# The last product of a transformer block, done as two column halves in two PSUM banks

## The chip, the cores and the metric

One core of a Trainium2 chip. The time is device microseconds of one execution, the median of several; in a trace the span from the first to the last instruction is some 2 us shorter. Engines: PE (TensorE) multiplies matrices, DVE (VectorE), ACT (ScalarE) and POOL (GpSimd) work elementwise, SP issues the transfers. PE writes into PSUM, which the kernel declares as 8 banks of 512 float columns. In the views L790 is line 790 of the kernel that ran, and a bracket says how long the engine had been idle before and what ended that.

## The reference, cut to what matters

```python
x = x + ga * _A_ref(h, A_wqkv, A_w_phi, A_wo)      # linear attention
h = _layernorm(x, axis=-1) * (1 + cb) + sb
x = x + gb * _B_ref(h, B_w1, B_w2)                 # relu(h @ w1) @ w2
```

x is 2048 x 576, the hidden layer 4608 wide. The change concerns only the last line: the second layer's product, the gate `gb`, and the residual addition.

## The kernel before: the parts that matter

The 2048 rows are 16 tiles of 128, worked in 8 passes of two. A pass forms its second-layer products in a scheme with partial products, which are summed in PSUM or through scratch copies (`SS`); the columns are in two parts of `HD = 288`. `fin` adds a saved partial sum, multiplies by the gate and adds the residual. Its scratch `yt` has one row of 288 floats for each column part:

```python
def fin(t, k, bank, s):
    c = slice(k * HD, (k + 1) * HD)
    y = yt[:, k, :]
    if s is None:
        dve.tensor_tensor(out=y, in0=PS[:, bank, 0:HD], in1=gb_row[:, c], op=ALU.mult)
    else:
        dve.tensor_tensor(out=y, in0=PS[:, bank, 0:HD], in1=SS[:, s, :], op=ALU.add)
        pool.tensor_tensor(out=y, in0=y, in1=gb_row[:, c], op=ALU.mult)
    pool.tensor_tensor(out=x_sb[:, t, c], in0=y, in1=x_sb[:, t, c], op=ALU.add)
```

The end of the last pass; t and t + 1 are its tiles:

```python
    fin(t + 1, 1, Z, 2)
    prod(X, A22, T4, al)
    fin(t + 1, 0, X, None)            # multiplies into yt[:, 0], POOL adds from there
    sp.dma_start(outf[(t + 1) * P:(t + 2) * P, :], x_sb[:, t + 1, :])
    ...                               # (passes before the last return here)
    rows, z = slice(t * P, (t + 1) * P), yt[:, 1, :]
    sp.dma_start(outf[rows, 0:HD], x_sb[:, t, 0:HD])
    pool.tensor_tensor(out=z, in0=SS[:, 1, :], in1=gb_row[:, HD:D], op=ALU.mult)
    pool.tensor_tensor(out=z, in0=z, in1=x_sb[:, t, HD:D], op=ALU.add)
    prod(Z, A12, B22, al)             # the last product: 18 matmuls of 288 columns
    dve.tensor_tensor(out=yt[:, 0, :], in0=PS[:, Z, 0:HD], in1=gb_row[:, HD:D], op=ALU.mult)
    dve.tensor_tensor(out=x_sb[:, t, HD:D], in0=yt[:, 0, :], in1=z, op=ALU.add)
    sp.dma_start(outf[rows, HD:D], x_sb[:, t, HD:D])
```

The softmax here doesn't subtract the row's maximum and nothing guards it: scores larger than these inputs give would overflow.

## Time and profile before

| | kernel before |
|---|---|
| time, first three runs | 392.11 us (391.75 to 392.55) |
| span of the profiled run | 390.7 us |
| PE busy | 98% |
| start of the last product | 384.42 us |
| end of the last product | 2.37 us after its start |
| last store issued | 3.56 us after its start |
| last instruction | 6.28 us after its start |

PE is full up to the end of the last product, so only the stretch behind it can be shortened by this change.

### The profile page before, as it was taken

The numbers are of one execution on the slowest core, as the hardware profiler recorded it, in microseconds if no ns is written. First come the engines' busy times: TensorE is split into PE (matmuls) and PEld (weight loads), VectorE is DVE, ScalarE is ACT, GpSimd is POOL, SyncE is SP. The second block draws the span as 40 slices with busy tenths as digits, with TensorE's granted clock in tenths as the row PEclk, the third lists the DMA queues.
The fourth block names the chain that finished last, engine by engine and source line by source line (L and its number), as shares of the span: only waits on it lengthen the run. The fifth ranks groups of instructions, "written<-read, shape, count | busy, mean of one in ns | idle before, by whom it ended". The sixth has DMA issues, their size and how long they took to land.

```text
span 390.7 us, 8908 instructions
## 1 busy us (share of the span) xinstructions
PE 383.8 (98%) x3693; PEld 311.7 (80%) x3693; DVE 244.3 (63%) x452; ACT 157.9 (40%) x360; POOL 142.3 (36%) x199
## 2 busy tenths in 40 slices
PE   8999999999999999999999999999999999999995
PEld 4778888878887888788888878887888788878874
DVE  0889998854879746573755567458555664653221
ACT  1798779699531233124213510531143123312510
POOL 2155858741101510740164045306510641072045
PEclk9999999999999999999999999999999999999999
DMA  7999739795732151125313311450143124010001
GB/s 291 418 420 403 274 133 354 178 306 161 189 65 35 47 121 20 35 61 109 35 27 83 80 35 32 107 65 19 47 93 35 24 69 51 18 34 33 3 0 32
DMA packets 49515, 44.36 MB, mean 114 GB/s; under 512 B 39361, under 2 KB 42050, under 8 KB 48706
## 3 DMA queue, kind: packets, MB, share of 16 engines
q1 hardware_dynamic: 49186, 43.59, 39.6%
q8 instruction: 29, 0.48, 0.5%
q10 hardware_dynamic: 288, 0.19, 0.2%
q14 instruction: 12, 0.10, 0.1%
HBM read 27.97 MB, written 6.49 MB: 88 GB/s over the span
## 4 chain that ended last, share of the span: by engine, by line
PE 86%; POOL 6%; ACT 2%; DVE 2%; DMA 2%; issue 1%; SPq 0%; POOLq 0%; DVEq 0%; ACTq 0%
PE PS L683 33%; PE PS L742 29%; PE PS L274 9%; PE PS L410 5%; PE PS L690 5%; POOL wo_sb L637 2%; PE PS L235 2%; PE PS L391 1%; ACT RT L279 1%; POOL RH L754 1%; DMA gatd<-gt 1%; PE PS L324 1%; POOL RT L291 1%; DMA ga_row<-gatd 1%; DVE st L240 1%
## 5 line engine op out<-in xcount | busy, mean ns | idle before, releaser
L683 PE MATMUL PS<-h,R 128*128 128x256 bf16 x1152 | 133.5, 273 | 0.0
L683 PEld LDWEIGHTS <-R 128*128 128x128 bf16 x1152 | 109.8, 98 | 17.5 <-issue 5.1
L742 PEld LDWEIGHTS <-RH 128*128 128x128 f16 x864 | 84.5, 98 | 21.8
L728 POOL TENSOR_TENSOR yt<-yt,gb_row 128x288 f32<-128x288 f32 x23 | 16.8, 731 | 167.0 <-DVE yt L727 167.0
L742 PE MATMUL PS<-R,RH 128*128 128x288 bf16 (+1 forms) x576 | 75.6, 286 | 0.0
L697 ACT ACTIVATE RH<-PS 128x256 f16<-128x256 f32 x72 | 27.7, 384 | 114.0 <-PE PS L690 107.4
L699 DVE SCALAR_TENSOR_TENSOR RH<-PS,RH 128x256 f16<-128x256 f32 x72 | 30.1, 419 | 68.2 <-ACT RH L697 68.2
L279 ACT ACTIVATE RT<-PS,rs 128x576 bf16<-128x576 f32 x64 | 43.0, 750 | 7.5 <-PE PS L274 7.1
L698 ACT ACTIVATE RH<-PS 128x512 f16<-128x512 f32 x72 | 42.9, 595 | 7.8 <-PE PS L683 6.5
L746 ACT ACTIVATE RS<-PS 128x288 f32<-128x288 f32 x24 | 9.9, 411 | 75.9 <-PE PS L742 75.9
L742 PE MATMUL PS<-RT,RH 128*128 128x288 f16 x288 | 37.9, 286 | 0.0
L274 PE MATMUL PS<-RH,R 116*128 116x288 bf16 x240 | 31.8, 286 | 0.5 <-ACT RH L631 0.5
L754 POOL TENSOR_TENSOR RH<-RH,RT 128x2304 f16<-128x2304 f16 x7 | 31.8, 4548 | 0.0
L274 PE MATMUL PS<-RH,RT 116*128 116x288 bf16 x240 | 31.7, 286 | 0.0
L274 PEld LDWEIGHTS <-R 116*128 116x128 bf16 x240 | 22.9, 98 | 6.4 <-issue 0.7
L274 PEld LDWEIGHTS <-RT 116*128 116x128 bf16 x240 | 22.7, 98 | 5.5
L420 DVE TENSOR_SCALAR xn<-x_sb,mv,rs 128x576 bf16<-128x576 bf16 (+1 forms) x28 | 22.4, 842 | 7.3 <-ACT rs L415 7.3
L729 POOL TENSOR_TENSOR x_sb<-yt,x_sb 128x288 bf16<-128x288 f32 x31 | 22.8, 737 | 5.9 <-DVE yt L725 4.1
L240 DVE BATCH_NORM_STATS2 st<-x_sb 128x6 f32<-128x288 bf16 x60 | 24.2, 445 | 0.5
L410 PE MATMUL PS<-wo_sb,oT 128*128 128x288 bf16 x160 | 22.6, 286 | 0.2 <-POOL wo_sb L637 0.2
L284 DVE TENSOR_REDUCE Rk<-RT 128x64 f32<-128x1152 bf16 x16 | 21.2, 1332 | 1.4 <-ACT RT L279 1.4
L284 DVE TENSOR_REDUCE Rq<-RT 128x64 f32<-128x1152 bf16 x16 | 21.5, 1342 | 0.0
(115 smaller groups left out, 414.2 us busy)
## 6 DMA issues: line engine op xcount, KB each, us to landing
R<-in_w1a_dram SPq DMA_DIRECT2D x4, 1152.0 KB
eqd<-RT SPq DMA_DIRECT2D x14, 288.0 KB, 5.8
RT<-eqd SPq DMA_DIRECT2D x14, 288.0 KB, 2.7
R<-in_w2a_dram SPq DMA_DIRECT2D x3, 864.0 KB, 10.4
R<-in_w2b_dram SPq DMA_DIRECT2D x2, 1296.0 KB, 10.9
out_dram<-x_sb SPq DMA_DIRECT2D x15, 144.0 KB, 3.3
RT<-in_xT_dram SPq DMA_DIRECT2D x2, 640.0 KB
x_sb<-in_xk_dram SPq DMA_DIRECT2D x3, 288.0 KB
```

The source lines that it names most:

```text
L240: dve.bn_stats(out=s[:, hf, :], in_=x_sb[:, t, hf * HD:(hf + 1) * HD])
L274: pe.matmul(pr[:, k, 0:HD], lhsT=xt(t, ck), rhs=w[0:R, ck, k * HD:(k + 1) * HD], start=(ck == 0), stop=(ck == NC - 1))
L279: act.activation(out=E.rearrange("p (b h s e) -> p b h s e", b=2, s=2, e=DH)[:, :, :, s, :], in_=pr[:, :, 0:HD].rearrange("p b (h e) -> p ...
L284: dve.tensor_reduce(out=Rr, in_=E.rearrange("p (c e) -> p c e", e=DH), axis=AXX, op=ALU.add)
L410: pe.matmul(pr[:, k, 0:HD], lhsT=oT[:, t % 2, ci, :], rhs=wo_sb[:, ci, k * HD:(k + 1) * HD], start=(ci == 0 and not add_x), stop=(ci == NC ...
L683: pe.matmul(PS[:, 2 * u + hf, n * 256:n * 256 + 256], lhsT=w1a[:, ci, jj * P:(jj + 1) * P], rhs=hb[:, ci, :], start=(n == 0 and ci == 0), ...
L697: act.activation(out=A11[:, j, :], in_=lo[:, :, 0, :], func=ACT.Relu)
L698: act.activation(out=A2[:, j, :, :], in_=PS[:, 2 * u + 1, :].rearrange("p (n s f) -> p n s f", n=2, s=2), func=ACT.Relu)
L699: dve.scalar_tensor_tensor(out=U3[:, j, :], in0=lo[:, :, 1, :], scalar=0.0, in1=A11[:, j, :], op0=ALU.max, op1=ALU.subtract)
L729: pool.tensor_tensor(out=x_sb[:, t, c], in0=y, in1=x_sb[:, t, c], op=ALU.add)
L742: pe.matmul(PS[:, bank, 0:HD], lhsT=am[:, j, :], rhs=bm[:, j, :], start=first and j == 0, stop=(j % 9 == 8), skip_group_check=True)
L754: pool.tensor_tensor(out=A12, in0=A12, in1=U2, op=ALU.subtract)
```

## The change

The intent: DVE can gate, add and release the first half of the columns while PE still works on the second, so that only half-width operations are left behind the last matmul. The second half goes to another bank; what the first bank already holds of its columns is therefore added beforehand, into a new buffer `yl` which also takes the saved partial sum, the gate and the residual. (The diff also moves an addition into a helper and adds default arguments, with the same operations as before.)

```diff
+    yl = RE[:, 0:2 * HD].bitcast(FP32)
...
         fin(t + 1, 1, Z, 2)
+        H4 = HD // 2
+        if b + 1 == NB:
+            dve.tensor_tensor(out=yl[:, H4:HD], in0=PS[:, Z, H4:HD], in1=SS[:, 1, H4:HD], op=ALU.add)
+            dve.tensor_copy(out=yl[:, 0:H4], in_=SS[:, 1, 0:H4])
+            pool.tensor_tensor(out=yl, in0=yl, in1=gb_row[:, HD:D], op=ALU.mult)
+            pool.tensor_tensor(out=yl, in0=yl, in1=x_sb[:, t, HD:D], op=ALU.add)
         prod(X, A22, T4, al)
         fin(t + 1, 0, X, None)
...
-        pool.tensor_tensor(out=z, in0=SS[:, 1, :], in1=gb_row[:, HD:D], op=ALU.mult)
-        pool.tensor_tensor(out=z, in0=z, in1=x_sb[:, t, HD:D], op=ALU.add)
-        prod(Z, A12, B22, al)
-        dve.tensor_tensor(out=yt[:, 0, :], in0=PS[:, Z, 0:HD], in1=gb_row[:, HD:D], op=ALU.mult)
-        dve.tensor_tensor(out=x_sb[:, t, HD:D], in0=yt[:, 0, :], in1=z, op=ALU.add)
+        for i, bank in enumerate((Z, 0)):
+            c, g = slice(i * H4, (i + 1) * H4), slice(HD + i * H4, HD + (i + 1) * H4)
+            for j in al:
+                pe.matmul(PS[:, bank, c], lhsT=A12[:, j, :], rhs=B22[:, j, c], start=(i == 1 and j == 0),
+                          stop=(j == NK - 1), skip_group_check=True)
+            dve.tensor_tensor(out=yt[:, 0, c], in0=PS[:, bank, c], in1=gb_row[:, g], op=ALU.mult)
+            dve.tensor_tensor(out=x_sb[:, t, g], in0=yt[:, 0, c], in1=yl[:, c], op=ALU.add)
```

More of the change, by code (lines that the diff above doesn't have):

```diff
@@ L403, in turn_dma, with wo_mm @@
         sp.dma_start_transpose(dst, src.rearrange("p (c f) -> p c f", f=P))
-    def wo_mm(t, pr, add_x):
+    def wo_mm(t, pr, add_x=False):
         for k in range(2):
@@ L411, in wo_mm, with add_res @@
                           start=(ci == 0 and not add_x), stop=(ci == NC - 1))
+    def add_res(t, pr):
+        x = v2(x_sb[:, t, :])
+        dve.tensor_tensor(out=x, in0=x, in1=pr[:, :, 0:HD], op=ALU.add)
     def ln2_rs(t):
@@ L415, in ln2_rs, with ln2_apply @@
         act.activation(out=rs2[:, t, 0:1], in_=lnv[:, t:t + 1], func=ACT.Exp, scale=-0.5)
-    def ln2_apply(t, src):
+    def ln2_apply(t, src=None):
         def cols(o, i):
@@ L771, in l2 @@
             return
-        rows, z = slice(t * P, (t + 1) * P), yt[:, 1, :]
+        rows = slice(t * P, (t + 1) * P)
         sp.dma_start(outf[rows, 0:HD], x_sb[:, t, 0:HD])
-        pool.tensor_tensor(out=z, in0=SS[:, 1, :], in1=gb_row[:, HD:D], op=ALU.mult)
-        pool.tensor_tensor(out=z, in0=z, in1=x_sb[:, t, HD:D], op=ALU.add)
-        prod(Z, A12, B22, al)
-        dve.tensor_tensor(out=yt[:, 0, :], in0=PS[:, Z, 0:HD], in1=gb_row[:, HD:D], op=ALU.mult)
-        dve.tensor_tensor(out=x_sb[:, t, HD:D], in0=yt[:, 0, :], in1=z, op=ALU.add)
+        for i, bank in enumerate((Z, 0)):
[5 more added lines that the diff above has]
+            dve.tensor_tensor(out=x_sb[:, t, g], in0=yt[:, 0, c], in1=yl[:, c], op=ALU.add)
         sp.dma_start(outf[rows, HD:D], x_sb[:, t, HD:D])
@@ L807, in in_l2 @@
                 pr = pair(i)
-                wo_mm(t, pr, False)
-                dve.tensor_tensor(out=v2(x_sb[:, t, :]), in0=v2(x_sb[:, t, :]), in1=pr[:, :, 0:HD], op=ALU.add)
+                wo_mm(t, pr)
+                add_res(t, pr)
                 bn(1, t)
@@ L814, in in_l2 @@
                 ln2_rs(t)
-                ln2_apply(t, None)
+                ln2_apply(t)
                 turn_dma(h2[:, (b + 1) % 2, :, i * P:(i + 1) * P], xn[:, t % 2, :])
```

## The prediction

> **What bounds the kernel now.** I read the busy shares first, then the 40 slices, then the timeline and the chain of waits of the last 10 us, because the change touches only the last product of the last of the eight passes. The page of the kernel before:
>
> ```profile
> span 390.7 us, 8908 instructions
> PE 383.8 (98%) x3693; PEld 311.7 (80%) x3693; DVE 244.3 (63%) x452; ACT 157.9 (40%) x360; POOL 142.3 (36%) x199
> PE   8999999999999999999999999999999999999995
> POOL 2155858741101510740164045306510641072045
> PE PS L683 33%; PE PS L742 29%; PE PS L274 9%; PE PS L410 5%; PE PS L690 5%; POOL wo_sb L637 2%; PE PS L235 2%; PE PS L391 1%; ACT RT L279 1%; POOL RH L754 1%; DMA gatd<-gt 1%; PE PS L324 1%; POOL RT L291 1%; DMA ga_row<-gatd 1%; DVE st L240 1%
> ```
>
> PE is full in every slice but the first and the last, and the chain is PE work nearly all the way. The change takes no work from PE. It can only shorten the stretch behind the last matmul, where PE is idle: that is the "5" of the last slice. The timeline of the end (start us, duration us, engine, line):
>
> ```profile
> 383.05 0.73 POOL L728 TENSOR_TENSOR yt<-yt,gb_row 128x288 f32<-128x288 f32 x1 [0.57 <-DVE yt L727]
> 383.86 0.73 POOL L729 TENSOR_TENSOR x_sb<-yt,x_sb 128x288 bf16<-128x288 f32 x1
> 384.42 2.37 PE L742 MATMUL PS<-R,RH 128*128 128x288 bf16 x18
> 384.69 0.46 DVE L725 TENSOR_TENSOR yt<-PS,gb_row 128x288 f32<-128x288 f32 x1 [1.72 <-POOL x_sb L729]
> 385.23 0.73 POOL L729 TENSOR_TENSOR x_sb<-yt,x_sb 128x288 bf16<-128x288 f32 x1 [0.64 <-DVE yt L725]
> 385.92 0.73 POOL L774 TENSOR_TENSOR yt<-RS,gb_row 128x288 f32<-128x288 f32 x1
> 385.98 0.33 SPq L766 DMA_DIRECT2D out_dram<-x_sb  x1
> 386.37 0.42 SPq L773 DMA_DIRECT2D out_dram<-x_sb  x1
> 386.73 0.73 POOL L775 TENSOR_TENSOR yt<-yt,x_sb 128x288 f32<-128x288 f32 x1
> 386.89 0.46 DVE L777 TENSOR_TENSOR yt<-PS,gb_row 128x288 f32<-128x288 f32 x1 [1.75 <-PE PS L742]
> 387.49 0.46 DVE L778 TENSOR_TENSOR x_sb<-yt 128x288 bf16<-128x288 f32 x1
> 387.98 0.33 SPq L779 DMA_DIRECT2D out_dram<-x_sb  x1
> ```
>
> The last product starts at 384.42 and ends at 386.79; DVE starts 0.10 us later. Behind it lie two DVE operations of 0.46 us, then the last store. The chain of waits for the same stretch:
>
> ```profile
> 385.96 0.69 POOL yt L774
> 386.65 0.04 issue
> 386.69 0.78 POOLq L924
> 387.46 0.02 issue
> 387.49 0.46 DVE x_sb L778
> ```
>
> So L778 was not released by DVE's own multiply (done at 387.35) but by POOL's addition L775 (386.73 + 0.73 = 387.46). In the tail two paths are nearly equal: PE through L777, and POOL through L774 and L775. After the store is issued at 387.98 there are 2.7 us to the end. The store queue's own waits put 1.3 us of these on the landing of the store, and its row gives 1.7 us from issue to landing for the two 72 KB stores; the remaining 1.0 us is the ending of the program. None of that is in the change.
>
> **What the Trainium skill says.** "TensorE: Matmul & The Clock Gate", section "Wait — 56ns, not 53.3ns?", gives for a warm array a start-to-start time of N / 2.4 GHz plus about 2.5 ns. The trace agrees: 18 matmuls of 288 columns take 2.37 us, the last 0.286 of it, so (2.37 - 0.286) / 17 = 122.6 ns against 122.5 by the formula. "PSUM — Partial Sum Buffer", section "PSUM bank collisions raise a hardware error", says that two engines may not touch one bank in the same partitions at once, not even at other columns. This is why the second half has to go to another bank; no run yet shows it. "VectorE: DVE Perf Modes", section "Mode 1× (REGULAR) — the baseline", gives one result per cycle, with 0.96 GHz in "Specifications". The trace agrees: the additions of 576 columns (L809) take 754 ns, those of 288 (L725) 458, so 296 / 288 = 1.03 ns per column. "DMA: Bandwidth & Descriptors", section "Queues, rings and completion order", says that each engine takes a queue's descriptors in ring order: a store issued close behind others stands behind their packets.
>
> **The change part by part.**
>
> PE: 18 matmuls of 288 columns become 36 of 144. The danger is the weight load, which is not halved but doubled in number. Its rows show 98 ns each, but they overlap: the 18 matmuls of 76 and 95 columns at L324, each with its own 128x128 load, take 0.86 us, so (0.86 - 0.2) / 17 = 39 ns per load and matmul. At 144 columns the columns therefore set the pace: 144 / 2.4 + 2.5 = 62.5 ns (an estimate from the first page, which the two sizes above confirm). The last starts at 384.42 + 35 x 0.0625 = 386.61 and takes some 0.226 us (76 columns 198 ns, 128 columns 220 ns, 288 columns 286 ns). PE ends at 386.84 instead of 386.79: **+0.05**. The first half is complete at 384.42 + 17 x 0.0625 + 0.226 = 385.71, so its two DVE operations lie beside the second half.
>
> DVE at the end: 144 columns instead of 288 save 144 x 1.03 = 148 ns each, so 458 becomes 310 ns. Start 386.84 + 0.10 = 386.94, first done 387.25, second some 0.03 later and done at 387.59, store possible at 387.62. The before had 387.98: **-0.36** from DVE's side, of which 0.11 is the removed wait for POOL and 0.30 the two shorter operations, less 0.05 for PE.
>
> DVE added: one addition of 144 columns out of PSUM (0.31 us) and a copy of 144 (about 0.2) at 383.0 to 383.5. DVE is idle there until 384.69: nothing on the path.
>
> POOL: the same two operations, but earlier in its queue, ahead of the addition for the first half of the tile before. Between independent operations starts are 0.69 us apart (385.23 to 385.92), between dependent ones 0.81 (383.05 to 383.86). New order: L728 383.05, L729 383.86, the new multiply 384.55, the new addition 385.36 (done 386.09), then the L729 that releases the first store at 386.05, done 386.78. Before it was done at 385.96: **that addition is 0.82 us later**, although DVE has its input ready at 385.15.
>
> SP: its queue is in order. The store of the tile before goes out at 386.80 (before: 385.98), the next after the same 0.39 us at 387.19, and the last no sooner than 387.19 + 0.48 = 387.67 (0.42 for the issue and 0.06 for the semaphore event that the trace has there). So the last store is ready at 387.62 by DVE and at **387.67 by the queue**: 0.31 us earlier than before instead of 0.36.
>
> Stores: L766's and L773's packets moved from about 386.6 to 387.7, which is up to 1.7 us after L766's issue; shifted, they end near 388.5. The last store's packets began about 0.7 us after its issue, so they would begin at 388.37 and stand behind the others for about 0.1 us. Before, a gap of 1 us lay between. I book **+0.1**.
>
> Sum: -0.31 + 0.1 = -0.2 us, so 392.11 - 0.2 = **391.9 us**.
>
> **The rivals.** (1) Only DVE counts, POOL and the stores are hidden: -0.36, some 391.75. For it speaks that the two stores are independent of the last one's data; against it the in-order queue, by a mere 0.05 us. (2) The weight load becomes the bound: if each narrow matmul took the 98 ns of its load row, PE would need 36 x 0.098 = 3.5 us instead of 2.3, and the time would go up by about 1.0, to 393.1. The 39 ns of L324 speak against it. (3) The stores collide fully: three of them issued within 0.9 us instead of 2.0, 288 KB together, and the last lands as late as before or later: 392.1 to 392.3. The slices at 300 to 390 GB/s say that the engines are nearly full only for some 0.5 us per store, so I give this a quarter. (4) Another wait, such as the first matmul of the second half for a reader of bank 0: that bank's last reader was the first layer at about 371, so it is free.
>
> **Range and chances.** The largest conceivable gain is the whole tail of DVE, under 1 us of 392, or 0.25%; the worst rival is +0.3%. Neither comes near 2%, which is 7.8 us. The three runs before spread 391.75 to 392.55, more than the effect. Range: -0.2 with about 0.45 to 0.5 to either side for the spread of medians, 391.4 to 392.4.
>
> **What would show it right or wrong.** In the changed trace: 36 matmuls at 62 to 63 ns, some 2.43 us in all; the two last DVE operations near 0.31 us each with no wait for POOL between them; the POOL addition of the tile before about 0.8 us later than now; its store issued near 386.8; the last store near 387.65, about 0.3 us earlier than 387.98, with the queue and DVE nearly tied; landing 1.7 to 1.9 us after issue. Wrong it is if the matmuls take over 70 ns, if PE waits between the halves, or if the store's landing grows by more than the tail shrinks.

## The result, and the profile after

The changed kernel took 391.73 us (391.54 to 392.26, 6 runs), the kernel before 392.32 us (6 runs). A ratio is the mean time of one kernel's fast runs over that of the other's in the same rounds, so it is not quite the ratio of these medians: here 0.9989, with a 95% interval of 0.9976 to 1.0002. The time lies within the predicted range, and the interval holds 1: no gain is shown. The trace says that the tail gained nothing. First, the timeline of the end of the changed kernel (start us, duration us, engine, line, operation):

```profile
382.09 0.77 DVE L772 COPY RE<-RS 128x144 f32<-128x144 f32 x1
...
383.41 2.41 PE L788 MATMUL PS<-R,RH 128*128 128x144 bf16 x36
383.53 0.73 POOL L773 TENSOR_TENSOR RE<-RE,gb_row 128x288 f32<-128x288 f32 x1
383.68 0.46 DVE L730 TENSOR_TENSOR yt<-PS,gb_row 128x288 f32<-128x288 f32 x1 [0.82 <-POOL x_sb L734]
384.35 0.73 POOL L774 TENSOR_TENSOR RE<-RE,x_sb 128x288 f32<-128x288 f32 x1
385.04 0.74 POOL L734 TENSOR_TENSOR x_sb<-yt,x_sb 128x288 bf16<-128x288 f32 x1
385.80 0.33 SPq L777 DMA_DIRECT2D out_dram<-x_sb  x1
385.80 0.31 DVE L790 TENSOR_TENSOR yt<-PS,gb_row 128x144 f32<-128x144 f32 x1 [1.67 <-POOL x_sb L734]
386.15 0.31 DVE L791 TENSOR_TENSOR x_sb<-yt,RE 128x144 bf16<-128x144 f32 x1
386.19 0.42 SPq L784 DMA_DIRECT2D out_dram<-x_sb  x1
386.37 0.30 DVE L790 TENSOR_TENSOR yt<-PS,gb_row 128x144 f32<-128x144 f32 x1
386.71 0.31 DVE L791 TENSOR_TENSOR x_sb<-yt,RE 128x144 bf16<-128x144 f32 x1
387.04 0.33 SPq L792 DMA_DIRECT2D out_dram<-x_sb  x1
```

The first L790 is the multiply of the first half. PE has this half complete early: 18 of 36 evenly spaced matmuls are through at about 1.3 us after the start of the product. Yet L790 starts at 385.80, which is 2.39 us after that start, at the time when PE finishes the second half too (383.41 + 2.41 = 385.82). Its bracket names the releaser: it was idle 1.67 us until POOL's L734 ended, at 385.04 + 0.74 = 385.78. Nothing runs beside the second half. All four half-width DVE operations stand behind the last matmul one after another, from 385.80 to 387.02, where before there were two of full width. The last store goes out 387.04 - 383.41 = 3.63 us after the start of the product, against 3.56 before.

Why should a multiply out of PSUM wait for POOL's addition for the other tile? L790 writes `yt[:, 0]`, and L734 reads `yt[:, 0]`: it is the addition of `fin(t + 1, 0, X, None)`, and the change put two POOL operations (L773, L774) ahead of it.

From the start of the last product to the last instruction it is 389.8 - 383.41 = 6.39 us, against 6.28. The tail became 0.1 us longer, while the span of the profiled run became 0.9 us shorter. That difference arose in the first 10 us, which the change leaves alone. The chain of waits at the beginning (start us, duration us, what), kernel before:

```profile
1.30 5.30 PE PS L235 x12
6.60 0.40 PE PS L251 x5
7.00 0.44 PE PS L235
```

and the changed kernel:

```profile
1.29 4.72 PE PS L235 x12
6.01 0.22 PE PS L251 x5
6.23 0.24 PE PS L235
```

The groups of L235 are matmuls on zeros that keep PE busy until the first data come; L251 is the first work on data. In the kernel before they ran slow for longer: 5.30 us instead of 4.72, and the next two groups took 0.84 instead of 0.46 us. The Trainium skill, "TensorE: Matmul & The Clock Gate", section "Part 1: The HAM clock gate (the "warmup" mystery)", says that PE's clock starts at half rate and is released at the end of a free-running window of about 3.4 us, so that the moment varies by some 500 ns from run to run. The trace agrees in kind: the same instructions, and 0.6 + 0.4 = 1.0 us of difference, which is the 1.0 us by which the last product started earlier. It does not agree in size: by the clock records of twelve traces the release came from 2.7 us (free_buffer) to 6.0 us (the kernel before) after the first of these matmuls, a spread of 3.3 us; in the two profiles compared here it was 6.0 and 4.0 us. The release is not all of the front either: in free_buffer and early_copy it came earliest, and PE then stood idle until the first data landed (in free_buffer 0.91 us, to 6.29).

### The profile page after: what moved, and what is told of

It is laid out like the page before. It is cut to its first block, busy times and chain, and to the rows that moved or that the text cites. A ratio compares the mean times of both kernels' runs of the same rounds, so it can differ in the third digit from the quotient of the medians.

```text
span 389.8 us, 8948 instructions
## 1 busy us (share of the span) xinstructions
PE 383.1 (98%) x3711; PEld 311.7 (80%) x3711; DVE 245.8 (63%) x456; ACT 157.8 (40%) x360; POOL 142.5 (37%) x199
## 4 chain that ended last, share of the span: by engine, by line
PE 87%; POOL 4%; DVE 4%; ACT 2%; DMA 1%; issue 1%; POOLq 0%; SPq 0%; DVEq 0%; ACTq 0%
PE PS L688 33%; PE PS L747 29%; PE PS L274 9%; PE PS L410 5%; PE PS L695 5%; PE PS L235 1%; PE PS L391 1%; ACT RT L279 1%; POOL RH L759 1%; PE PS L324 1%; POOL RT L291 1%; DVE RT L479 1%; DMA gatd<-gt 1%; DVE st L240 1%; DMA ga_row<-gatd 1%
## 5 line engine op out<-in xcount | busy, mean ns | idle before, releaser
L747 PEld LDWEIGHTS <-RH 128*128 128x128 f16 x846 | 82.7, 98 | 21.3
L747 PE MATMUL PS<-R,RH 128*128 128x288 bf16 (+1 forms) x558 | 73.2, 286 | 0.0
L734 POOL TENSOR_TENSOR x_sb<-yt,x_sb 128x288 bf16<-128x288 f32 x31 | 22.7, 735 | 5.3 <-DVE yt L730 3.5
```

The source lines that it names most:

```text
L747: pe.matmul(PS[:, bank, 0:HD], lhsT=am[:, j, :], rhs=bm[:, j, :], start=first and j == 0, stop=(j % 9 == 8), skip_group_check=True)
```

## The experiments

**Theory.** The gain is lost because the first half's multiply waits to overwrite a scratch row that POOL reads late; the earlier start in the first profile came from the varying front. **Rivals.** The tail did gain, and the 0.1% is its gain; or DVE waited for something else; or the split is worth nothing in itself, the moved preparation being all. All numbers marked "after S" are counted from the start of the last product in the run's own trace.

| run | S us | last store issued after S | last instruction after S | ratio to before (95% interval) |
|---|---|---|---|---|
| kernel before, first profile | 384.42 | 3.56 | 6.28 | |
| before_again | 383.87 | 3.55 | 6.23 | 0.9997 (0.9985 to 1.001) |
| change, first profile | 383.41 | 3.63 | 6.39 | 0.9989 (0.9976 to 1.0002) |
| change_again | 383.46 | 3.64 | 6.44 | 1.0 (0.9988 to 1.0013) |
| free_buffer | 383.92 | 3.28 | 6.38 | 1.0001 (0.9987 to 1.0015) |
| pool_order | 383.28 | 3.96 | 6.92 | 1.0009 (0.9995 to 1.0023) |
| store_order | 384.04 | 3.13 | 6.16 | 0.9998 (0.9985 to 1.001) |
| no_split | 383.54 | 3.45 | 6.16 | 0.9989 (0.9975 to 1.0002) |
| partials_on_dve | 383.65 | 3.13 | 5.85 | 0.9987 (0.9975 to 1.0) |
| uneven_split | 383.37 | 3.03 | 5.93 | 0.9982 (0.9969 to 0.9994) |
| uneven_again | 383.59 | 3.03 | 5.81 | 0.9973 (0.996 to 0.9987) |
| early_copy (one look) | 383.43 | 3.29 | 6.97 | |

All outputs are right.

### The two kernels once more

before_again and change_again have no edit.

> The kernel before once more, unchanged, timed against itself. Theory: the 1.0 us by which the changed kernel's profile reached its last product earlier (383.4 against 384.4 us) is the varying warm-up of TensorE's clock at the start, so even two copies of one kernel differ by some 0.1 to 0.2% in a profile, and the ratio's interval holds 1. Within the tail nothing moves: the last store is issued 3.56 us after the start of the last product. Rival: the front of one kernel is steady to 0.1 us, and then the 1.0 us belongs to the change.

> The changed kernel once more. Theory (its tail is no shorter, the gain of 0.1% was the front): last store issued 3.63 us after the start of the last product, as in its first profile, and a ratio to the kernel before between 0.999 and 1.001. Rival (the split gains 0.2 to 0.3 us as predicted): ratio 0.9985 to 0.9993 again, in every round.

The kernel before, timed against itself, reached its last product 0.55 us earlier than in its first profile (383.87 against 384.42), with its tail the same to 0.01 us at the store. The changed kernel repeated its 3.64 us and this time came out at a ratio of 1.0. So the front of one and the same kernel varies by more than the whole effect sought, and the tail, measured from S, repeats; the rival that the front is steady and the 1.0 us belongs to the change falls. This is how a change of 0.1% can be read at all: by intervals within a trace. The tail of the changed kernel is longer by 0.08 us at the store and by 0.1 to 0.2 us at the end, in two profiles of two.

### The other scratch row

```diff
-            dve.tensor_tensor(out=yt[:, 0, c], in0=PS[:, bank, c], in1=gb_row[:, g], op=ALU.mult)
-            dve.tensor_tensor(out=x_sb[:, t, g], in0=yt[:, 0, c], in1=yl[:, c], op=ALU.add)
+            dve.tensor_tensor(out=yt[:, 1, c], in0=PS[:, bank, c], in1=gb_row[:, g], op=ALU.mult)
+            dve.tensor_tensor(out=x_sb[:, t, g], in0=yt[:, 1, c], in1=yl[:, c], op=ALU.add)
```

> The changed kernel, but the two halves' products with the gate go to the other row of the scratch buffer, which POOL has read by then. Theory (the first half waited for POOL to read the scratch row that it overwrites): the first half's multiply starts about 1.4 us after the start of the last product instead of 2.39, its addition ends by 2.1, the second half follows PE at once, and the last store is issued at about 3.26 us (held by the store queue; DVE would be ready at 3.18) instead of 3.63. Rival (DVE waited for something else that POOL does, or for PE): first multiply stays at 2.39, store at 3.63.

The timeline of this run, from the first half's multiply on; S is 383.92:

```profile
385.31 0.31 DVE L790 TENSOR_TENSOR yt<-PS,gb_row 128x144 f32<-128x144 f32 x1 [0.67 <-PE PS L788]
385.54 0.73 POOL L734 TENSOR_TENSOR x_sb<-yt,x_sb 128x288 bf16<-128x288 f32 x1
385.73 0.71 DVE L791 TENSOR_TENSOR x_sb<-yt,RE 128x144 bf16<-128x144 f32 x1
...
387.20 0.41 SPq L792 DMA_DIRECT2D out_dram<-x_sb  x1
```

The multiply now starts 1.39 us after S, is released by PE and not by POOL, and is done (385.62) while POOL's addition still runs (to 386.27). The last store is issued at 3.28 us. One index of a buffer gives back 0.36 us at the store: the theory stands, and the rival (another cause of the wait) falls. One detail was missed: the first half's addition, expected to end by 2.1 us, took 0.71 instead of 0.31 us and ended at 2.52, 0.17 us after POOL's L734, beside which it ran; the second half's multiply still followed PE by 0.04 us. And the run as a whole won nothing, ratio 1.0001, and the last instruction is 6.38 us after S. By the trace's completion records the last store landed 1.68 us after its issue (1.61 in both kernels; 0.07 us of the difference is the issue itself, 0.41 instead of 0.33 us). After that, the end of the program took 1.4 us instead of 1.1 to 1.2. The instructions named DRAIN in DVE's queue, the last of which belongs to the ending, show it (durations ns min/median/max, first and last start us), the changed kernel:

```profile
L937 DVEq DRAIN  x2: 19/182/345, 386.7 to 389.3; - x2
```

and free_buffer:

```profile
L937 DVEq DRAIN  x2: 120/234/347, 386.7 to 389.9; - x2
```

DVE's last drain takes 120 ns instead of 19, and it comes 389.9 - 387.20 = 2.7 us after the issue of the last store instead of 389.3 - 387.04 = 2.3. The store queue's longest wait for PE in the ending rose from 0.4 to 0.7 us with it. Two more kernels have this (store_order, pool_order), the other six do not, early_copy among them, which differs from free_buffer only in the place of one copy. What decides it I did not find; it stays open.

### POOL's order alone

```diff
-            pool.tensor_tensor(out=yl, in0=yl, in1=gb_row[:, HD:D], op=ALU.mult)
-            pool.tensor_tensor(out=yl, in0=yl, in1=x_sb[:, t, HD:D], op=ALU.add)
         prod(X, A22, T4, al)
         fin(t + 1, 0, X, None)
+        if b + 1 == NB:
+            pool.tensor_tensor(out=yl, in0=yl, in1=gb_row[:, HD:D], op=ALU.mult)
+            pool.tensor_tensor(out=yl, in0=yl, in1=x_sb[:, t, HD:D], op=ALU.add)
```

> The changed kernel with POOL's two preparing operations put back behind its addition for the tile before; the scratch row is still the shared one. Theory: the overwrite wait ends early (that addition is done about 1.5 us after the start of the last product instead of 2.37), so the first half's multiply starts at about 1.55; but the prepared rest is then ready only at about 3.0, the first half's addition waits for it, and the second half's operations stand behind it in DVE's order: the last store at about 4.0 us, later than 3.63. Rival (the overwrite wait is all that matters): store at 3.2.

The timeline of this run; S is 383.28:

```profile
384.09 0.73 POOL L734 TENSOR_TENSOR x_sb<-yt,x_sb 128x288 bf16<-128x288 f32 x1 [0.64 <-DVE yt L730]
...
384.85 0.31 DVE L791 TENSOR_TENSOR yt<-PS,gb_row 128x144 f32<-128x144 f32 x1 [0.84 <-POOL x_sb L734]
...
386.35 0.31 DVE L792 TENSOR_TENSOR x_sb<-yt,RE 128x144 bf16<-128x144 f32 x1 [1.19 <-POOL RE L777]
```

The multiply again waits for POOL's L734, but this is over 0.8 us earlier, so it starts 1.57 us after S. Its addition then waits 1.19 us for the prepared rest, and the second half's operations stand behind it in DVE's order: store at 3.96. Both POOL results are needed early, and POOL can give only one of them first. With the scratch row shared, each order has its own wait.

### The preparation on DVE

free_buffer, and further:

```diff
-            dve.tensor_copy(out=yl[:, 0:H4], in_=SS[:, 1, 0:H4])
-            pool.tensor_tensor(out=yl, in0=yl, in1=gb_row[:, HD:D], op=ALU.mult)
-            pool.tensor_tensor(out=yl, in0=yl, in1=x_sb[:, t, HD:D], op=ALU.add)
+            dve.tensor_tensor(out=yl[:, 0:H4], in0=SS[:, 1, 0:H4], in1=gb_row[:, HD:HD + H4], op=ALU.mult)
+            dve.tensor_tensor(out=yl[:, H4:HD], in0=yl[:, H4:HD], in1=gb_row[:, HD + H4:D], op=ALU.mult)
+            dve.tensor_tensor(out=yl, in0=yl, in1=x_sb[:, t, HD:D], op=ALU.add)
```

> As free_buffer, and the two POOL operations and the copy that prepare the rest are three short DVE operations (0.3, 0.3 and 0.46 us) in DVE's idle time ahead of the last product. Theory: POOL's addition for the tile before starts at about 0.8 us after the start of the last product instead of 1.63, its store at 1.55 instead of 2.39, the store queue is free at 2.45, and the last store is issued when DVE is ready, at 3.2 us. Rival (the new DVE operations with two SBUF inputs are held up by POOL's and push back the multiply for the tile before): POOL's addition at 1.2 or later, the last store still at 3.2 to 3.3.

The rival's detail was right in kind, and it did not matter. Two of the new operations took 0.84 and 0.87 us beside POOL work, and POOL's addition for the tile before began 1.10 us after S, where the theory had 0.8 and the rival 1.2 or later. The last store still went out at 3.13, because the first half was done with time to spare. The last instruction came 5.85 us after S, 0.4 us earlier than in the kernel before; the ratio, 0.9987, just touches 1.

### The preparation without the split

The kernel before, with `z` moved to `RE` and its two operations given to DVE ahead of the last two products:

```diff
         fin(t + 1, 1, Z, 2)
+        z = RE[:, 0:2 * HD].bitcast(FP32)
+        if b + 1 == NB:
+            dve.tensor_tensor(out=z, in0=SS[:, 1, :], in1=gb_row[:, HD:D], op=ALU.mult)
+            dve.tensor_tensor(out=z, in0=z, in1=x_sb[:, t, HD:D], op=ALU.add)
...
-        pool.tensor_tensor(out=z, in0=SS[:, 1, :], in1=gb_row[:, HD:D], op=ALU.mult)
-        pool.tensor_tensor(out=z, in0=z, in1=x_sb[:, t, HD:D], op=ALU.add)
```

> The kernel before with only the preparation of the rest moved from POOL to DVE's idle time ahead of the last product; the product stays whole, 18 matmuls of 288 columns. Theory: the 0.1 us wait for POOL goes and nothing else, so the last store is issued at about 3.45 us after the start of the last product, against 3.56 before and 3.13 in partials_on_dve: the split itself is then worth 0.3 us. Rival (the gain of partials_on_dve is the moved preparation): 3.1 to 3.2 here too.

Store at 3.45, as the theory said: the wait for POOL in the kernel before was worth 0.11 us, and the split, once it is unhindered, 3.45 - 3.13 = 0.32 us. The timed ratio, 0.9989, cannot tell this run from partials_on_dve; the trace can.

### The order of the stores

free_buffer, with the store of the tile's first 288 columns put ahead:

```diff
+        if b + 1 == NB:
+            sp.dma_start(outf[t * P:(t + 1) * P, 0:HD], x_sb[:, t, 0:HD])
         sp.dma_start(outf[(t + 1) * P:(t + 2) * P, :], x_sb[:, t + 1, :])
...
-        sp.dma_start(outf[rows, 0:HD], x_sb[:, t, 0:HD])
```

> free_buffer, with the store of the first 288 columns of the last tile (ready long before) put ahead of the tile before's store in the store queue. In free_buffer the last store was issued 3.28 us after the start of the last product while DVE was done at 3.10 to 3.15. Theory (the in-order queue held it by some 0.1 us): now it is issued at 3.13 to 3.18, as soon as DVE is done. Rival (DVE alone sets it): 3.28 again. Also looked at: whether the end of the program again takes 1.4 us from landing to the last instruction, as in free_buffer, or 1.1 as in the others.

Store at 3.13: in free_buffer the in-order queue had held it for 0.15 us. The ending was the long one again, so the ratio is 0.9998.

### An uneven split

partials_on_dve with the early store first, and 192 and 96 columns:

```diff
-        H4 = HD // 2
+        H4 = 192
...
-            c, g = slice(i * H4, (i + 1) * H4), slice(HD + i * H4, HD + (i + 1) * H4)
+            c = (slice(0, H4), slice(H4, HD))[i]
+            g = (slice(HD, HD + H4), slice(HD + H4, D))[i]
```

> partials_on_dve, split in 192 and 96 columns, with the early store first in the queue. Theory: PE needs as long (18 x 82.5 + 18 x 42.5 ns), the last two DVE operations cost about 0.26 us each instead of 0.31, so the last store is issued at about 3.03 us after the start of the last product instead of 3.13, and the time is some 0.5 us under the kernel before (ratio 0.9987). Rival (at 96 columns the weight load sets the pace, or DVE is still busy with the first half when the second is complete): PE takes longer than 2.41 us, or the store is at 3.13 or later.

> uneven_split once more, to see whether a version that beats the kernel before is there in fact. Theory: ratio 0.998 to 0.9995 again, last store at 3.03 us after the start of the last product. Rival (its 0.9982 was the varying front): ratio at 1.000 or above.

The end of uneven_split's timeline; S is 383.37:

```profile
385.82 0.26 DVE L792 TENSOR_TENSOR yt<-PS,gb_row 128x96 f32<-128x96 f32 x1
386.12 0.26 DVE L793 TENSOR_TENSOR x_sb<-yt,RE 128x96 bf16<-128x96 f32 x1
386.40 0.33 SPq L794 DMA_DIRECT2D out_dram<-x_sb  x1
```

PE again takes 2.41 us for its 36 matmuls, now of two widths, so a weight load at 96 columns does not set the pace. The last two operations cost 0.26 us each, and the store goes out at 3.03. The early store is not what gains against partials_on_dve: there the queue was free at 386.38 (386.32 and 0.06 us for the event), before DVE was done at 386.76. In both submissions this kernel was faster than the kernel before, with an interval that excludes 1: 0.9982 and 0.9973. By the trace some 0.4 us (0.1%) of it belong to the tail; the rest of the second figure is of the size of the front's variation. So this version is faster than the kernel before, by far less than 2%. Against the changed kernel it was never timed in the same rounds; its tail is shorter, 3.03 against 3.63 us at the store.

### What held up a copy

The copy of 144 columns in the changed kernel took 0.77 us, where the prediction had 0.2. It ended 0.09 us after a POOL operation, which suggested that it had been held. For a test, free_buffer with the copy placed ahead of the addition before it, inside POOL's long subtraction:

```diff
+        if b + 1 == NB:
+            dve.tensor_copy(out=yl[:, 0:H4], in_=SS[:, 1, 0:H4])
         fin(t + 1, 1, Z, 2)
...
-            dve.tensor_copy(out=yl[:, 0:H4], in_=SS[:, 1, 0:H4])
```

> free_buffer, with the copy of 144 columns moved ahead of the addition before it, where POOL is in its long subtraction (4.54 us, ending 1.95 us before the start of the last product). In free_buffer the copy took 0.77 us and ended 0.08 us after a POOL operation. Theory (a DVE copy within on-chip memory can't run beside a POOL operation and is held until that ends): the copy begins about 6 us before the last product, as soon as ScalarE has written its source, and lasts some 4 us, to the end of POOL's subtraction. Rival (0.77 us is the cost of such a copy): 0.77 us here too, or less. The last store stays at 3.28 us under both.

The two operations of this run:

```profile
376.94 4.55 POOL L759 TENSOR_TENSOR RH<-RH,RT 128x2304 f16<-128x2304 f16 x1
...
377.46 4.12 DVE L770 COPY RE<-RS 128x144 f32<-128x144 f32 x1 [2.09 <-ACT RS L751]
```

The same copy took 4.12 us and ended at 381.58, 0.09 us after POOL (381.49). Its length is POOL's, not its own. This agrees with the Trainium skill, "SBUF — State Buffer", section "SBUF: two separate sides": DVE and POOL share a pair of ports under an exclusive lock, which a DVE operation needs in a two-port mode (a float copy within SBUF runs in one) or with two inputs in SBUF; the loser waits for the whole instruction of the other. In this run the store was issued at 3.29, as expected, but the store queue then waited 2.2 us in all for the last stores to land, against 1.2 in free_buffer, which is why its last instruction comes 6.97 us after S: the last store landed 2.61 us after its issue, against 1.68 in free_buffer, though both issue it 0.51 us behind the store before. One look does not say why.

## Why the prediction was right or wrong

The number was right, the path to it was not. That the time came out is luck: the expected gain of 0.2 us was smaller than the run-to-run spread for which the range allowed, and the varying front covered a tail that had become longer.

- **PE: right.** 36 matmuls took 2.41 us (predicted 2.43), that is (2.41 - 0.226) / 35 = 62.4 ns each. The rival with the weight load as the bound is refuted (its sum compares with 2.3 us where the product takes 2.4; this changes nothing).
- **DVE's last operations: right in size.** 0.30 to 0.31 us each.
- **POOL's order: right.** Its addition for the tile before ended 2.37 us after S; the prediction's 386.78 - 384.42 is 2.36.
- **"The first half is complete at ... 385.71, so its two DVE operations lie beside the second half": wrong, and this is the step that failed.** The data were complete, but the output row was not free. The prediction had computed that POOL's addition would end 0.82 us later, and followed this only to the store that it releases, not to the buffer that it reads. The multiply started at 2.39 instead of 1.39 us after S; two operations more fell behind the last matmul (its rival 4 did think of another wait, but of PE's, for a PSUM bank); and the last store was issued at 3.63 instead of the predicted 387.67 - 384.42 = 3.25 us. free_buffer, with this one wait gone, gave 3.28.
- **The store queue: right, once it could be seen.** In free_buffer it held the last store for 0.15 us, which store_order took away. In the changed kernel itself DVE was later than the queue.
- **The +0.1 for crowding stores: not seen in the changed kernel, open where stores crowd.** The row's 1.7 us, which the prediction read for both 72 KB stores, is that of the first; the last one landed 1.61 us after its issue in both kernels. But in the changed kernel it came 0.85 us behind the store before, not the predicted 0.48. At 0.51 us it landed after 1.68 us in free_buffer, about what was booked, and after 2.61 us in the single look at early_copy, so the rival that the stores collide is not excluded for that spacing.
- **The sum:** -0.2 was predicted for the tail, and +0.1 to +0.2 was measured in it. The time moved the other way in the first round (391.73) and not at all in the second (ratio 1.0); in the profiled runs the front, with the clock's release, explains the difference, and for the runs without a profile this is inferred.
- **The copy's 0.2 us:** it was 0.77, held by POOL; off the path, so without effect.

## What to carry to other kernels

When work is moved earlier to overlap, list for each operation not only what it reads but which buffer it overwrites, and who still reads that; a reordering on one engine (here two POOL operations) delays the reader and with it the overwriter. Where the expected gain is smaller than the variation of the whole, measure it as an interval within the trace from a fixed event, and run the unchanged kernel against itself. Once this tail was free of waits, the width of the last elementwise operations set when the last store was issued, and a narrow last part gained more than halves did (3.03 against 3.13 us).

## What the Trainium skill lacked or had wrong

- "TensorE: Matmul & The Clock Gate" calls the warm-up's effect under 1% of a typical span; true here as well. Its spread of some 500 ns for the release is too small here: 3.3 us over twelve traces. And no page draws the consequence for measuring small changes: starts of the last product differed by 1.14 us (383.28 to 384.42) over these profiles, of which the 1.0 us between the first two profiles lay in the first 10 us.
- "DMA: Bandwidth & Descriptors" gives its fit of about 2.0 us of fixed cost for transfers issued through GpSimd and none for stores from SP: here the last store of 72 KB landed 1.60 to 1.76 us after its issue, data included, in the ten profiles where it was issued 0.75 us or more behind the store before. Three stores within 0.9 us brought 1.68 us in free_buffer and 2.61 us in early_copy; no page gives a size for this.
- No page says why one program's ending is longer than another's: from the landing of the last store to the last instruction it took 1.1 to 1.2 us in nine profiles and 1.4 in three, where DVE's closing drain took 120 to 138 ns instead of 19. The cause stays open.
- "SBUF — State Buffer" states the port lock, and no run contradicts it; the size to keep in mind is that a copy of 144 columns took 4.12 us beside a POOL operation of 4.55 us.
